# A planner that counts device-memory transfers as longer, and loads that come behind the query unit's pass

## The chip, the cores and the metric

The kernel runs on one core of one Trainium2 chip. The metric is the time of the program on the device in microseconds; the median of several executions counts. Engines are named as in the profile: PE (TensorE, matmuls), PEld (its weight loads), DVE (VectorE), ACT (ScalarE), POOL (GpSimd) and SP (SyncE, which issues all transfers here).

## The reference

Inputs q, k, v have 8 batches, 8 heads, 576 positions and 64 features, in fp32; w_phi is 64 x 128.

```
def phi(x):
    proj = einsum('bhsd,df->bhsf', x, w_phi)
    proj = proj - max(abs(proj), axis=-1)
    return concatenate([exp(proj), exp(-proj)], axis=-1)
q_p, k_p = phi(q), phi(k)
kv  = einsum('bhsf,bhsd->bhfd', k_p, v);  z = sum(k_p, axis=2)
att = einsum('bhsf,bhfd->bhsd', q_p, kv) / (einsum('bhsf,bhf->bhs', q_p, z) + 1e-6)
x   = att as 4608 tokens x 512          # heads side by side
h   = x @ w_in                          # 512 x 2048
out = (h * tanh(softplus(h))) @ w_out   # Mish, then 2048 x 512
```

## The kernel before, in words

Two things run interleaved on one core: linear attention, and the two matrix products with Mish between them.

The 4608 tokens are cut into 18 chunks of 256 (`NCH`, `CH`). For each chunk there are 16 input tiles (`ff_in`, L435: 12 matmuls each, since weight and x are each split into a high and a low part), 8 Mish steps on pairs of tiles (`mish`, L448), the low part of the result (`g_low`, L457) and 16 output tiles (`ff_out`, L470). An input-tile pair writes one of two banks of h; Mish reads it and so frees it.

Attention is cut into units of 512 columns: 36 key units (`k0`...) and 36 query units (`q{chunk}_{g}`). A key unit is loaded (`load_raw`, L250), projected (`project`, L260), centred on VectorE (`centre`, L268), exponentiated on ScalarE (`k_exp`, L322) and summed with v into kv (`k_sum`, L327). Each of the 32 pairs p of heads has its own v (`load_v`, L313). A query unit is loaded, projected and centred likewise. Its features must then be turned over: for the first three chunks by TensorE transposes (`q_turn`), from chunk 3 on (`NTURNED`, query unit 6 on) by a pass through device memory: VectorE regroups 32 x 32 blocks (`q_regroup`), SP sends 256 KB to a scratch tensor (`q_send`, L297) and fetches it back turned in four transfers of 64 KB (`q_fetch`, L302), for each of the two halves j of the unit. Exponentials (`q_exp`, L355), products with kv (`q_num`), the division (`q_divide`) follow, and the result x makes the same pass (`x_regroup`, `x_send`, `x_fetch`), after which ScalarE casts its high part (`q_high`, L423) and VectorE forms its low part (`q_low`, L429). A chunk's first input tile needs x of both its units.

A step takes one query unit and, five steps ahead, one key unit: in step n, projection of query unit n and key unit n + 5, and 8 input and 8 output tiles.

The order of the instructions on each engine isn't that of the code. The class `Plan` (L48) makes it. Each task has an engine, a key (its priority), an assumed duration `took`, an assumed delay `late` until others see its end, tasks it depends on (`deps`: they must have ended; `after`: they must only have been issued), and ring slots that it takes and gives back. `order` (L60) plays the program through in assumed time: a free engine takes the ready task with the lowest key, ScalarE preferring within 1.5 of key one that needs no other activation table. The sequence of issue is then the program's order; each engine runs its instructions in that order, and on the chip waits for what each really needs. For transfers the planner keeps a bus: `size` bytes at 400 KB per assumed microsecond, with a start delay, and a least time until the data count as landed (L104 to L106). SP's `took` is 0.42 for one transfer and 1.68 for the four of a fetch.

The first loads and the weights' tasks have handwritten keys (`FIRST_KEYS`, `FIRST_QUERIES`, `WKEYS`); from query unit 6 on keys come from `step_time` (L504), 8 to a step. `unit_tasks` (L515) adds the load, projection and centring of a unit.

Of the kernel before, what the change touches and what calls it, by code (L numbers as in the profile page):

```python
# [24 lines left out]
NCH = NTOK // CH  # L25
# [9 lines left out]
NTURNED, NTHERE, EARLY, RAMP = 3, 8, 2.042, (5, 4)  # L35

NK, LEAD = B * NHP * S // 512, 5
# [10 lines left out]
class Plan:  # L48
# [4 lines left out]
    def add(self, name, engine, key, took, fn, deps=(), take=(), give=(), late=0.15, table=None, size=0,  # L53
            after=()):
        task = dict(name=name, engine=engine, key=key, took=took, fn=fn, deps=deps, take=take, give=give, late=late,
                    table=table, size=size, after=after, seq=len(self.tasks))
        self.tasks.append(task)
        self.named[name] = task

    def order(self):  # L60

        waiting = {}
        for task in sorted(self.tasks, key=lambda t: (t["key"], t["seq"])):
            waiting.setdefault(task["engine"], []).append(task)
        free = dict.fromkeys(waiting, 0.0)
        done, slots, released = {}, {}, {}
        now, table, bus = 0.0, None, 2.5
        issued = []

        def ready(task):  # L70
            if any(dep not in done for dep in task["after"]):
                return False
            for dep in task["deps"]:
                if done.get(dep, 1e9) > now:
                    return False
            for ring, _ in task["take"]:
                held_now = sum(released.get(token, 1e9) > now for token in slots.setdefault(ring, []))
                if held_now + sum(r == ring for r, _ in task["take"]) > self.rings.get(ring, 1):
                    return False
            return True  # L80

        while any(waiting.values()):
            moved = False
            for engine, queue in waiting.items():
                if free[engine] > now or not queue:
                    continue
                found = None
                for task in queue[:48]:
                    if found and task["key"] > found["key"] + 1.5:
                        break  # L90
                    if not ready(task):
                        continue
                    if found is None:
                        found = task
                    if task["table"] in (None, table):
                        found = task if found["table"] not in (None, table) else found
                        break
                if found is None:
                    continue
                took, late = found["took"], found["late"]  # L100
                if found["table"] not in (None, table):
                    table = found["table"]
                    took += 1.29
                if found["size"]:  # L104
                    bus = max(bus, now + 0.9) + found["size"] / 400e3
                    late = max(bus - now, 1.9) - took  # L106
                for ring, token in found["take"]:
                    slots[ring] = [t for t in slots[ring] if released.get(t, 1e9) > now]
                    slots[ring].append(token)
                free[engine] = now + took  # L110
                done[found["name"]] = now + took + late
                for token in found["give"]:
                    released[token] = now + took + late
                issued.append((now, len(issued), found))
                queue.remove(found)
                moved = True
            if not moved:
                times = [t for t in list(free.values()) + list(done.values()) if t > now + 1e-9]
                if not times:
                    raise RuntimeError("the plan is stuck: " + ", ".join(q[0]["name"] for q in waiting.values() if q))  # L120
                now = min(times)
        return [task for _, _, task in issued]
# [3 lines left out]
def attention_then_mish(ctx, tc, qT, kT, va, w_phi, w_in, w_out, out):  # L126
# [123 lines left out]
    def load_raw(unit, home, src):  # L250
        slot, half = home
        if half is None:
            raws[unit] = work.tile([P, 512], F32, tag="raw", name=f"raw_{unit}", bufs=NRAW)
        else:
            if half == 0:
                shared[slot] = slot_tile(slot, F32, f"raw_{unit}")
            raws[unit] = shared[slot][:, half, :]
        nc.sync.dma_start(raws[unit], src)
# [54 lines left out]
    def load_v(p):  # L313
        if p < NHP:
            vt = spare_tile(NRAWSPARE // 2 + p, F32, f"v_{p}").rearrange("p a b -> p (a b)")
            vt = vt[:, :10 * VW].rearrange("p (t j w) -> p t j w", t=5, j=2)
        else:
            vt = work.tile([P, 5, 2, VW], F32, tag="v", name=f"v_{p}", bufs=NV)
        nc.sync.dma_start(vt.rearrange("p t j w -> p (t j w)"), va[p])
        vs[p] = vt  # L320
# [186 lines left out]
    add = plan.add  # L507
# [7 lines left out]
    def unit_tasks(unit, step, t, load, src, kinds, size):  # L515
        home, e_homes = raw_home(), [e_home(), e_home()]
        slot, half = home
        token = f"raw:{unit}" if half is None else f"{slot}:{shared_by.setdefault(slot, unit)}"
        take = [] if half == 1 else [(slot, token)]
        add(f"load {unit}", "SP", load, 0.42, lambda: load_raw(unit, home, src), take=take, size=size)  # L520
        last_use.setdefault(slot, []).append(f"project {unit}")
        for h in e_homes:
            last_use.setdefault(h, []).append(f"sum {unit}" if unit[0] == "k" else f"num {unit} 1")
        add(f"project {unit}", "PE", t, 1.0, lambda: project(unit, kinds), deps=[f"load {unit}"], after=sums_at.get(step - 1, ()),
            take=[(kind, f"pp{j}:{unit}") for j, kind in enumerate(kinds)], give=[token] if half != 0 else [])
        add(f"centre {unit}", "DVE", t, 2.4, lambda: centre(unit, e_homes), deps=[f"project {unit}"],
            take=[(h, f"e{j}:{unit}") for j, h in enumerate(e_homes)], give=[f"pp{j}:{unit}" for j in range(2)])

    shared_by, last_use, sums_at = {}, {}, {}
    units = sorted([(t, 0, n) for n, t in key_time.items()] + [(t, 1, n) for n, t in query_time.items()])  # L530
    for t, is_query, n in units:
        steady = t >= query_time[NFIRST]
        first = t < 0
        load = (-40.0 + t if t < -3 else -46.6 + 0.2 * t) if first else t - 4.0
        exps = (t + 8 * E0, t + 8 * (E0 + E1)) if steady else (t + 0.3, t + 0.5)
        sums = step_time((n if is_query else n - LEAD) + 1) - 0.03 if steady else t + 1.0
        if not is_query:
            unit = f"k{n}"
# [4 lines left out]
            deps, take, give, ends = [f"exp {unit} 0", f"exp {unit} 1"], [], [], []  # L543
            cost = 0.1
            for i in range(4):
                for p, slot in pairs_of(4 * n + i):
                    cost += 0.466
                    if slot == 0:
                        take.append(("o" if p < NHP else "att", f"kvps:{p}"))
                        vslot = spare[NRAWSPARE // 2 + p] if p < NHP else "v"  # L550
                        add(f"load v{p}", "SP", load + 0.3, 0.42, lambda p=p: load_v(p), take=[(vslot, f"v:{p}")], size=337920)
                        deps.append(f"load v{p}")
                    if slot == 4:
                        last_use.setdefault(spare[NRAWSPARE // 2 + p] if p < NHP else "v", []).append(f"sum {unit}")
                        ends.append(p)
                        give.append(f"v:{p}")
# [7 lines left out]
        else:  # L564
            c, g = divmod(n, 2)
            unit = f"q{c}_{g}"
# [3 lines left out]
            for j in range(2):  # L570
                if by_dma:
                    add(f"regroup {unit} {j}", "DVE", t + 0.1, 0.68, lambda c=c, g=g, j=j: q_regroup(c, g, j), deps=[f"centre {unit}"])
                    add(f"send {unit} {j}", "SP", t + 0.3, 0.42, lambda c=c, g=g, j=j: q_send(c, g, j), deps=[f"regroup {unit} {j}"],
                        size=262144)
                    add(f"turn {unit} {j}", "SP", t + 0.8, 1.68, lambda c=c, g=g, j=j: q_fetch(c, g, j), deps=[f"send {unit} {j}"],
                        size=262144)
# [3 lines left out]
                turn = exps[j] if steady else t + 0.1 + 0.1 * j  # L580
                add(f"turn {unit} {j}", "PE", turn, 0.4, lambda c=c, g=g, j=j: q_turn(c, g, j), deps=[f"centre {unit}"],
                    take=[("att", f"dt{j}:{unit}")])
# [4 lines left out]
            for i in range(2):  # L587
                pair = 2 * g + i
                if steady:
# [3 lines left out]
                    take=[("att", f"num{i}:{unit}")],  # L593
# [11 lines left out]
            else:  # L605
                add(f"out {unit}", "PE", outs, 0.4, lambda c=c, g=g: q_out(c, g), deps=[f"divide {unit} {i}" for i in range(2)],
                    take=[("att", f"xt:{unit}")], give=[f"x:{unit}"])
# [5 lines left out]
    for i, pc in enumerate(pieces):  # L613
# [5 lines left out]
        if i < nmiddle:  # L619
            home = homes[i % len(homes)]  # L620
# [3 lines left out]
        def split(step, took, fn, deps, **more):  # L624
# [5 lines left out]
              take=[("part", f"rest:{nm}"), ("half", f"t:{nm}")] if own else [])  # L630
# [11 lines left out]
    for n in range(total):  # L642
        c, f = tiles[n]
        deps = [f"{s} {('in', cc, f // 4)}" for cc in range(NCC) for s in ("ready", "split")] + [f"low q{c}_{g}" for g in range(2)]
        add(f"in {c} {f}", "PE", n, 1.405, lambda c=c, f=f: ff_in(c, f), deps=deps + ([before_in] if before_in else []),
            take=[] if f % 2 else [("h", f"h:{c}_{f // 2}")], give=[f"xT:q{c}_{g}" for g in range(2)] if f == NFT - 1 else [])
        before_in = f"in {c} {f}"
        if f % 2:
            fp = f // 2
            add(f"mish {c} {fp}", "ACT", n + 0.01, 1.05, lambda c=c, fp=fp: mish(c, fp), deps=[before_in],  # L650
                take=[("u", f"u:{c}_{fp}"), ("g", f"g0:{c}_{fp}"), ("g", f"g1:{c}_{fp}")], give=[f"h:{c}_{fp}"], table="mish")
            add(f"low {c} {fp}", "DVE", n + 0.02, 0.67, lambda c=c, fp=fp: g_low(c, fp), deps=[f"mish {c} {fp}"], give=[f"u:{c}_{fp}"])
        part, first, end = part_of(c, f)
        if f == end - 1:
# [6 lines left out]
            take=[("o", f"o{tt}:{c}_{part}") for tt in range(2)] if f == first else [], give=gives)  # L661
        before_out = f"out {c} {f}"
        if f == end:
            for tt in range(2):
                final = f == NFT - 1
                on_act = c == NCH - 1 and final and not tt or part == 0 and not final
                if part == 0 and not final:
                    take = [("part", f"part{tt}:{c}")]
# [44 lines left out]
```

## Time and profile before

| | |
|---|---|
| median of 3 runs | 1114.09 us (1109.9 to 1115.74) |
| the profiled execution | 1113.29 us |
| its span, first to last instruction | 1111.5 us |
| granted TensorE clock, mean | 0.993 |
| mean DMA rate over the span | 108 GB/s |
| x sends (`there_x`), median from issue to landing | 3.0 us |
| e_q sends (`there_e`), median from issue to landing | 2.2 us |
| raw_k loads, median from issue to landing | 2.9 us |
| v loads, median from issue to landing | 3.7 us |

The page gives for each engine its busy time and share of the span; the stretches give the same for parts of the span (busy us and instructions of PE, PEld, DVE, ACT, POOL, then the granted clock, the DMA engines' share and GB/s). A line of the waits names the waiting engine, its tile and line, the one that it waited for, and then the total in us, the number of times and the longest. A line of a timeline has start and duration in us, engine, source line, operation, output, input, shapes, how many were merged, and in brackets the idle time before it and what ended it.

### The profile page before, as it was taken

Reading aid. Unit: us, or ns where it says so; the run is one execution under the profiler, and the core shown is the slowest. Engines: PE = TensorE matmul, PEld = TensorE weight load, DVE = VectorE, ACT = ScalarE, POOL = GpSimd, SP = SyncE. Lnnn points to the kernel's source line nnn. Section 1 sums busy time; section 2 is a strip of 40 time slices with the busy share of each in tenths; the row PEclk is TensorE's granted clock in tenths of the full one; section 3 lists DMA queues with packets and bytes.
Section 4 is the critical chain, followed back from the end, with each engine's and each line's share of the span. In section 5 each row is a group of like instructions: output and inputs, shape, how many; then the busy total and the mean of one; then the engine's idle time right before and its main releaser. Section 6 shows DMA issues by size and latency. Waiting matters only on the chain.

```text
span 1111.5 us, 26782 instructions
## 1 busy us (share of the span) xinstructions
PE 1074.4 (97%) x11272; PEld 963.0 (87%) x11272; DVE 537.2 (48%) x1184; ACT 657.7 (59%) x1007; POOL 0.7 (0%) x6
## 2 busy tenths in 40 slices
PE   7799999999999999999999999999999999999998
PEld 7689988998898888888888988889899988999887
DVE  7899996444444444333444444444444443433211
ACT  6498996555555556666666665566666563443422
POOL 0000000000000000000000000000000000000000
PEclk9899999999999999999999999999999999999999
DMA  9568743233332322222232322232322221322100
GB/s 352 190 228 287 268 137 105 77 109 108 89 108 89 102 65 88 80 81 88 77 108 89 108 89 96 85 104 77 103 74 93 88 85 58 99 78 76 44 21 19
DMA packets 94008, 120.10 MB, mean 108 GB/s; under 512 B 10432, under 2 KB 56640, under 8 KB 93888
## 3 DMA queue, kind: packets, MB, share of 16 engines
q1 hardware_dynamic: 93888, 118.38, 32.5%
q8 instruction: 89, 1.46, 0.5%
q14 instruction: 31, 0.25, 0.1%
HBM read 85.31 MB, written 33.03 MB: 106 GB/s over the span
## 4 chain that ended last, share of the span: by engine, by line
PE 64%; ACT 14%; DMA 10%; DVE 6%; SPq 3%; issue 3%; ACTq 0%; DVEq 0%
PE h L445 24%; PE o L480 23%; PE kvps L289 7%; PE num L289 6%; DMA there_x<-via 4%; ACT L451 3%; DMA x<-there_x 3%; SPq L302 2%; PE pp_q L266 2%; DMA e_q<-there_e 2%; PE pp_k L266 2%; ACT L355 2%; ACT u L451 1%; ACT e_k L324 1%; ACT L324 1%
## 5 line engine op out<-in xcount | busy, mean ns | idle before, releaser
L445 PE MATMUL h<-xTh,win 128*128 128x256 f32 x2304 | 463.9, 284 | 19.0 <-ACT u L451 16.4
L445 PEld LDWEIGHTS h<-xTh,win 128*128 128x128 f32 x2304 | 374.3, 189 | 45.7 <-ACT u L451 28.8
L480 PE MATMUL o<-wout,gh 128*128 128x512 f32 x1152 | 363.7, 397 | 0.2 <-ACT wout L234 0.2
L445 PE MATMUL h<-xTl,win 128*128 128x256 f32 x1152 | 325.1, 282 | 0.9 <-DVE xTl L429 0.9
L462 DVE TENSOR_TENSOR gl<-u,gh 128x256 fp32r<-128x256 f32 x288 | 110.0, 422 | 420.6 <-ACT gh L454 402.5
L480 PE MATMUL o<-wout,gl 128*128 128x512 f32 x576 | 227.2, 394 | 0.0
L445 PEld LDWEIGHTS h<-xTl,win 128*128 128x128 f32 x1152 | 216.8, 188 | 10.4 <-DVE xTl L429 1.5
L480 PEld LDWEIGHTS o<-wout,gh 128*128 128x128 f32 x1152 | 197.7, 188 | 30.0 <-ACT wout L234 0.6
L451 ACT ACTIVATE u<-h 128x512 f32<-128x512 f32 x144 | 86.1, 598 | 104.4 <-PE h L445 88.7
L423 ACT CAST xTh<-x 128x512 fp32r<-128x512 f32 x30 | 18.7, 622 | 199.6 <-DMA x<-there_x 199.6
L480 PEld LDWEIGHTS o<-wout,gl 128*128 128x128 f32 x576 | 108.3, 188 | 26.4
L451 ACT ACT_TABLE_LOAD x91 | 116.8, 1283 | 1.6
L454 ACT CAST gh<-u 128x256 fp32r<-128x256 f32 x288 | 104.1, 405 | 6.1
L324 ACT ACT_TABLE_LOAD x36 | 46.2, 1283 | 87.3 <-DVE e_k L281 86.8
L289 PEld LDWEIGHTS kvps<-v,e_k 128*64 128x64 f32 x2560 | 79.5, 139 | 8.6 <-issue 5.5
L289 PE MATMUL kvps<-v,e_k 128*64 128x66 f32 x2560 | 84.4, 225 | 0.7 <-issue 0.6
L289 PE MATMUL num<-kv,e_q 128*64 128x66 f32 x2304 | 76.8, 225 | 0.5 <-ACT e_q L360 0.5
L289 PEld LDWEIGHTS num<-kv,e_q 128*64 128x64 f32 x2304 | 72.6, 140 | 4.1 <-issue 1.8
L355 ACT ACT_TABLE_LOAD x42 | 53.9, 1283 | 9.5 <-DMA e_q<-there_e 8.8
L429 DVE TENSOR_TENSOR xTl<-x,xTh 128x512 fp32r<-128x512 f32 x30 | 20.8, 693 | 63.8 <-ACT xTh L423 63.8
L273 DVE TENSOR_REDUCE m_k<-pp_k 128x4 f32<-128x512 f32 x72 | 46.1, 681 | 8.8 <-PE pp_k L266 8.7
L324 ACT ACTIVATE e_k<-e_k 128x512 f32<-128x512 f32 x72 | 45.1, 626 | 6.5 <-DVE e_k L281 6.1
(59 smaller groups left out, 774.9 us busy)
## 6 DMA issues: line engine op xcount, KB each, us to landing
there_e<-e_q SPq DMA_DIRECT2D x60, 256.0 KB, 2.2
e_q<-there_e SPq DMA_DIRECT2D x240, 64.0 KB, 2.0
v<-va SPq DMA_DIRECT2D x32, 330.0 KB, 3.7
raw_q<-qT SPq DMA_DIRECT2D x36, 256.0 KB, 3.2
out<-osb SPq DMA_DIRECT2D x36, 256.0 KB, 2.3
raw_k<-kT SPq DMA_DIRECT2D x35, 256.0 KB, 2.9
words_in<-w_in SPq DMA_DIRECT2D x16, 512.0 KB, 5.9
words_out<-w_out SPq DMA_DIRECT2D x16, 512.0 KB, 4.9
```

The source lines that it names most:

```text
L266: nc.tensor.matmul(ps[j][:, n], raw[rows, n * P:(n + 1) * P], w_phi2[rows], start=True, stop=True)
L273: nc.vector.tensor_reduce(ms[j], ps[j], axis=AX.X, op=ALU.max, apply_absolute_value=True)
L289: nc.tensor.matmul(ps[rows], lhsT[h], rhs[h], start=start, stop=stop, skip_group_check=True)
L302: nc.sync.dma_start(dst[32 * b:32 * b + 32].rearrange("i (a m) -> i a m", a=4), src[:, b * P:(b + 1) * P].rearrange("(a i) m -> i a m", a=4))
L324: nc.scalar.activation(e[:, 1, :], e[:, 0, :], AF.Exp)
L355: nc.scalar.activation(e[:, 1, :], e[:, 0, :], AF.Exp)
L429: nc.vector.tensor_sub(natural(lo), xt_ps.pop((c, g)), natural(hi).bitcast(F32))
L445: nc.tensor.matmul(ps, w[:, wcol], x[:, cc % 2, :], start=(n == 0), stop=(n == 11))
L451: nc.scalar.activation(u, h_live.pop((c, fp)).rearrange("p f s -> p (f s)"), AF.Mish)
L454: nc.scalar.copy(gh, u[:, f * CH:(f + 1) * CH])
L462: nc.vector.tensor_sub(gl, u[:, f * CH:(f + 1) * CH], gh.bitcast(F32))
L480: nc.tensor.matmul(ps, g[:, cols], w, start=(i == first and k == 0), stop=(i == end and k == 2))
```

## The change

The planner's cost of a transfer is changed in two numbers: the bus starts it 1.0 after its issue in place of 0.9, and the data count as landed no sooner than 2.4 after the issue's end (`took`), where it was 1.9 after the issue's start. Nothing else in the planner is touched. And loads of raw inputs and of v get an `after`: from step 7 to step 35 they may be issued only when the second fetch (j = 1) of the query features of the step before has been issued. Loads of weights, and sends and fetches themselves, get no `after`.

```
-                    bus = max(bus, now + 0.9) + found["size"] / 400e3
-                    late = max(bus - now, 1.9) - took
+                    bus = max(bus, now + 1.0) + found["size"] / 400e3
+                    late = max(bus - now - took, 2.4)
...
-        add(f"load {unit}", "SP", load, 0.42, lambda: load_raw(unit, home, src), take=take, size=size)
+        add(f"load {unit}", "SP", load, 0.42, lambda: load_raw(unit, home, src), take=take, size=size, after=turned_at(step - 1))
...
+    def turned_at(step):
+        return [f"turn q{step // 2}_{step % 2} 1"] if 2 * NTURNED <= step < 2 * NCH else []
...
-                        add(f"load v{p}", "SP", load + 0.3, 0.42, lambda p=p: load_v(p), take=[(vslot, f"v:{p}")], size=337920)
+                        add(f"load v{p}", "SP", load + 0.3, 0.42, lambda p=p: load_v(p), take=[(vslot, f"v:{p}")], size=337920,
+                            after=turned_at(n - LEAD - 1))
```

## The prediction

> **What bounds the kernel now.** I read the page's busy shares and chain first, then the waits, then the stretches of the span, then the timelines of two steps that behave differently.
>
> ```profile
> span 1111.5 us, 26782 instructions
> ...
> PE 1074.4 (97%) x11272; PEld 963.0 (87%) x11272; DVE 537.2 (48%) x1184; ACT 657.7 (59%) x1007; POOL 0.7 (0%) x6
> ...
> PE 64%; ACT 14%; DMA 10%; DVE 6%; SPq 3%; issue 3%; ACTq 0%; DVEq 0%
> ```
>
> TensorE has work for all but 37.1 us of the span (1111.5 - 1074.4), so no change of order can win more than that. Yet a quarter of the chain that ended last is ACT and DMA (14% and 10%). The waits say where those touch TensorE:
>
> ```profile
> ACT xTh L423 <- DMA x<-there_x: 199.6, 30, 12.6
> ...
> PEld h L445 <- ACT u L451: 28.8, 31, 2.2
> ...
> PE h L445 <- ACT u L451: 16.4, 22, 1.7
> ...
> PE h L445 <- DVE xTl L429: 0.9, 3, 0.3
> ```
>
> ScalarE sits 199.6 us, 30 times, in front of the cast of x, waiting for x to come back from device memory. Whatever is written behind that cast in ScalarE's order waits with it, Mish (L451) too, and TensorE's input tiles wait 31 times for Mish, because Mish frees the bank of h that they write. The stretches show that this isn't everywhere:
>
> ```profile
> 20.00:40.00 20.00, 17.81 (x395) 16.39 (x390) 15.02 (x40) 9.69 (x18) 0.00 (x0) 0.91 0.58 217
> 40.00:60.00 20.00, 14.78 (x192) 13.78 (x191) 18.32 (x45) 12.01 (x20) 0.00 (x0) 0.83 0.74 255
> ...
> 400.00:500.00 100.00, 96.33 (x1113) 86.12 (x1112) 43.60 (x98) 58.05 (x88) 0.00 (x0) 1.00 0.28 85
> ...
> 800.00:900.00 100.00, 100.00 (x1025) 90.44 (x1024) 43.24 (x92) 63.94 (x93) 0.00 (x0) 1.00 0.30 95
> ```
>
> From 400 to 500 TensorE is idle 3.67 us, from 800 to 900 not at all, with the same kind of steps in both. The difference is in the order. A step of the first kind, by SyncE's, VectorE's, ScalarE's and TensorE's timelines:
>
> ```profile
> 528.61 0.35 SPq L258 DMA_DIRECT2D raw_k<-kT  x1
> 529.11 0.34 SPq L297 DMA_DIRECT2D there_x<-via  x1
> 529.63 0.33 SPq L258 DMA_DIRECT2D raw_q<-qT  x1
> 532.08 1.75 SPq L302 DMA_DIRECT2D x<-there_x  x4
> ...
> 536.88 3.64 SPq L302 DMA_DIRECT2D e_q<-there_e  x8
> ```
> ```profile
> 528.37 0.71 DVE L293 STREAM_TRANSPOSE via<-x 128x512 f32<-128x512 f32 x1
> ...
> 532.57 1.27 DVE L281 TENSOR_TENSOR e_k<-pp_k,m_k 128x512 f32<-128x512 f32 x2
> ...
> 537.00 0.69 DVE L429 TENSOR_TENSOR xTl<-x,xTh 128x512 fp32r<-128x512 f32 x1 [1.95 <-ACT xTh L423]
> ```
> ```profile
> 536.35 0.62 ACT L423 CAST xTh<-x 128x512 fp32r<-128x512 f32 x1 [11.48 <-DMA x<-there_x]
> 536.99 1.28 ACT L324 ACT_TABLE_LOAD   x1
> 538.28 0.64 ACT L324 ACTIVATE e_k<-e_k 128x512 f32<-128x512 f32 x1
> 538.95 0.63 ACT L325 ACTIVATE e_k<-e_k 128x512 f32<-128x512 f32 x1
> 539.60 1.28 ACT L451 ACT_TABLE_LOAD   x1
> 540.89 0.60 ACT L451 ACTIVATE u<-h 128x512 f32<-128x512 f32 x1
> ...
> 547.35 0.60 ACT L451 ACTIVATE u<-h 128x512 f32<-128x512 f32 x1
> ```
> ```profile
> 505.20 0.40 PE L480 MATMUL o<-wout,gl 128*128 128x512 f32 x1
> 505.44 0.28 PE L445 MATMUL h<-xTh,win 128*128 128x256 f32 x1
> ...
> 540.65 0.40 PE L480 MATMUL o<-wout,gl 128*128 128x512 f32 x1
> 541.54 0.39 PE L445 MATMUL h<-xTh,win 128*128 128x256 f32 x1 [0.50 <-ACT u L451]
> ...
> 547.05 0.39 PE L480 MATMUL o<-wout,gl 128*128 128x512 f32 x1
> 548.00 0.39 PE L445 MATMUL h<-xTh,win 128*128 128x256 f32 x1 [0.56 <-ACT u L451]
> ```
>
> VectorE ends the regroup of x at 529.08 (528.37 + 0.71); the cast runs at 536.35, 7.27 us later. The exponentials of the key unit were ready from 533.84 (532.57 + 1.27) and stood behind the cast. An unhindered change from output to input matmuls takes 0.24 us from start to start (505.20 to 505.44); here it takes 0.89 and 0.95, so this step loses 0.65 + 0.71 = 1.36 us. The row's own 0.50 and 0.56 are too small, since a matmul's recorded duration covers part of the gap. The weight loads' row is too large by about 0.28 each (its wait at 547.99 is 0.99 for a loss of 0.71), so the whole loss is 28.8 - 31 x 0.28 = 20.1 us.
>
> The Trainium skill ("Perfetto Trace Analysis", section "Identifying the Most-Contended Engine") holds that matmul busy time is a poor measure of headroom and that the busy share of weight loads should be taken. By that rule 148.5 us (1111.5 - 963.0) would be open to a change. The trace doesn't bear that out for a change of order: between 800 and 900 nothing waits and weight loads still stand at 90.44%.
>
> A step of the second kind:
>
> ```profile
> 564.47 0.70 DVE L293 STREAM_TRANSPOSE via<-x 128x512 f32<-128x512 f32 x1
> ```
> ```profile
> 564.04 1.28 ACT L324 ACT_TABLE_LOAD   x1 [8.77 <-DVE e_k L281]
> ...
> 570.52 0.62 ACT L423 CAST xTh<-x 128x512 fp32r<-128x512 f32 x1 [1.24 <-DMA x<-there_x]
> ...
> 658.76 0.62 ACT L423 CAST xTh<-x 128x512 fp32r<-128x512 f32 x1 [2.33 <-DMA x<-there_x]
> ```
> ```profile
> 660.16 0.38 PE L445 MATMUL h<-xTl,win 128*128 128x256 f32 x1 [0.23 <-DVE xTl L429]
> ```
>
> Here exponentials and a Mish stand ahead of the cast, ScalarE waits only 1.24 us for x, and TensorE doesn't wait for Mish. The pass took 5.35 us (565.17 to 570.52). In exchange x comes just in time where it opens a new chunk (660.16, 0.23 us late).
>
> **The change part by part.** The planner's numbers decide only the order in which each engine's instructions are written; the times below are the trace's.
>
> *Transfers counted as longer.* Before, a 256 KB transfer with the bus free is planned as done 1.9 us after its issue, so send and fetch take 3.8 us. Now it is its issue time plus 2.4: 0.42 + 2.4 = 2.82 for a send, 1.68 + 2.4 = 4.08 for a fetch, together 6.9 us. The chip takes 7.27 in the first kind of step and 5.35 in the second, so the old plan was short by 3.5 and 1.6 us, and the new one is off by -0.4 and +1.6.
>
> What the planner then puts ahead of the cast is what is ready in those 3.1 us: the table load with the first exponential pair (1.28 + 0.64 + 0.63 = 2.55 us), or the Mish that is due. In the step shown ScalarE would start the pair at 533.84 and end it at 536.4, just when x is there; the cast follows to 537.0, the table load for Mish to 538.3. Mish runs at about 538.4 instead of 540.89, 2.5 us earlier. What is late next is the following Mish: 6.46 us separate the two (540.89 to 547.35), because table loads and exponentials lie between, while TensorE needs one per two tile pairs, 5.75 us (548.00 - 541.54, less the 0.71 it waited). So ScalarE loses 0.7 us of its lead per such cycle, and 2.5 us hold for this step. The longest single loss in the trace is 2.2 - 0.28 = 1.9 us, below that lead. I credit 19 of the 20.1 us.
>
> What it may cost: at a chunk's first input tile x has no time in hand in steps of the second kind. If the cast stands behind another pair, 2.55 us, of which ScalarE spends 2.33 idle anyway (658.76), the cast is about 0.2 us late; with a fetch planned longer than it is, up to 1.6 us later. Fifteen chunks begin that way, at 0 to 1.6 us each; most steps of the first kind have 541.54 - 537.69 = 3.85 us in hand and pay nothing. I take 2 us in all, bounds 0 and 24. For such cycles that bunch up (0.7 us each) I take another 2, bounds 0 and 10.
>
> *The same numbers in the ramp.* The first 60 us are bound by arrivals and by handwritten keys: idle 2.19 and 5.22 us in the two stretches above. There a raw load is now planned 0.92 us later (2.82 for 1.9), a weight piece 0.6 later (2.82 for 2.21) when the bus is free.
>
> ```profile
> words_in<-w_in SPq DMA_DIRECT2D x16, 512.0 KB, 5.9
> raw_q<-qT SPq DMA_DIRECT2D x36, 256.0 KB, 3.2
> ```
>
> Both really land later than either plan says, so the new order should be nearer the truth, but no row shows what it will be. Bounds: half of the two idle stretches won, -4 us; two tile pairs of 2.8 us delayed, +6. I take 0.
>
> *Loads behind the query unit's pass.* From step 7 on raw q, raw k and v are loaded after the second fetch of the query features of the step before. The loads leave their place around the send of x (528.61 and 529.63 around 529.11; the fetch that needs the landing starts at 532.08, 2.97 us after the send). SyncE's queue: what they pass is the send and fetch of x, the two sends and eight fetch instructions of e_q; no load's wait for a projection then stands in front of these. Cost: in each step they are issued some 12 us later, at 540.5 (536.88 + 3.64). They are used by the next projection:
>
> ```profile
> 558.18 1.16 PE L266 MATMUL pp_q<-w_phi,raw_q 64*128 64x128 f32 x16
> ```
>
> 540.5 + 3.2 is 543.7, so 14 us remain, and I cost the move at nothing; without that cover each step would pay up to 3.2 us. Its gain, x some 0.9 us sooner, goes into ScalarE's lead and isn't counted again; bounds 0 and 1.
>
> The Trainium skill says the contrary of this move ("DMA: Bandwidth & Descriptors", section "Rules for kernel authors"): issue a transfer early and wait for it late, so that its fixed cost is hidden. By that rule the later issue is a loss. The trace shows it still hidden by 14 us, so both come to nothing here.
>
> **Sum.** -19 + 2 + 2 + 0 = -15 us on the profiled execution's 1113.29 us (span 1111.5 and 1.8 around it): 1098.3. That execution lies 0.8 below the median of 1114.09, so I forecast 1099.0.
>
> **The rivals.** *Same time: the loss comes back elsewhere.* ScalarE needs 6.46 us for a Mish with a table turn, TensorE 5.75. If query features, now planned 3.1 us later, make three turns out of two in a step, 0.7 us in each of 30 steps gives 21 us back against 19, and where only half the steps do it, 10: 1104 to 1116. For it: from 536.35 to 541.49 ScalarE runs without a gap in the step shown. Against it: from 800 to 900 the same work goes by without idle time on TensorE.
>
> *Slower: x comes too late for its chunk.* If the longer plan puts a further table turn ahead of the cast in steps of the second kind, the first input tile of a chunk waits 2.55 us, 15 times: +38 - 19 = +19, so 1133. It decides once the cast is over 1.3 us late per chunk on average (19 / 15). For it: 660.16 shows no time in hand. Against it: x is ready at a lower key than the second exponential pair, and a cast needs no table, so the planner prefers it; and in the first kind 3.85 us are free.
>
> *The change does nothing.* If the planner's order on ScalarE stays, because TensorE's own pace decides when tasks are ready, only x's 0.9 us remain: a gain below 0.65 us per step in some 14 steps, 1105 to 1114.
>
> **How the numbers follow.** Forecast 0.6, with its own range 1091 to 1107 (all of the 20 us and a ramp 4 better; half of it and a ramp worse). Loss comes back 0.15; nothing 0.1; slower 0.15. The range takes the forecast, both middle cases and the lesser part of the slow one: 1091 to 1121. A measurement here can tell 0.5%, 5.6 us, from no change: faster is below 1108.5, which holds the forecast and some of both middle cases (0.04), 0.64; slower is above 1119.7, the slow rival and a ramp that goes wrong without a gain behind it (0.02), 0.17; the rest is 0.19.
>
> **What would show it.** Right: ScalarE's wait at the cast falls from 199.6 us to under 60, with exponentials or Mish ahead of it in every step; input tiles wait for Mish under 10 times over 0.35 us; TensorE's idle time from 200 to 1050 falls by over 10 us; the raw loads stand behind the eight fetches on SyncE, and fetches of x start about 2 us after the send. Wrong: long waits of input tiles for VectorE's low part of x (the slow rival), ScalarE without a gap but TensorE still waiting for Mish (loss comes back), or a first 170 us that is longer by more than the rest wins.

## The result, and the profile after

The changed kernel takes 1082.85 us (median of 4 runs, 1081.57 to 1083.76) against 1112.53 us before (4 runs, 1109.9 to 1115.74): a ratio of 0.9731 with a 95% interval of 0.97 to 0.9762, so 29.7 us less. The forecast had the direction and the place, but half the size: 1099.0, some 15 us less, with a range that ended at 1091.

The page of the changed kernel, the lines that answer to those shown of before (busy time of the engines, and the chain that ended last):

```profile
span 1080.5 us, 26883 instructions
...
PE 1061.9 (98%) x11272; PEld 963.2 (89%) x11272; DVE 539.9 (50%) x1184; ACT 666.3 (62%) x1013; POOL 0.7 (0%) x6
...
PE 89%; ACT 6%; DVE 3%; issue 1%; DMA 1%; SPq 0%; ACTq 0%; DVEq 0%
```

TensorE is now 89% of the chain (64% before), and DMA went from 10% to 1%. Note that TensorE's busy time fell too, by 12.5 us, though it runs the same 11272 matmuls: part of what was lost before had been counted as busy. The waits of the changed kernel:

```profile
ACT L324 <- DVE e_k L281: 201.9, 22, 10.0
...
ACT xTh L423 <- DMA x<-there_x: 15.2, 10, 3.1
...
PEld h L445 <- ACT u L451: 1.5, 1, 1.5
```

ScalarE's wait for x fell from 199.6 us to 15.2. ScalarE still idles, but now mostly in front of the key unit's exponentials (201.9 us), at a time when no Mish is due: in the step shown below the pair of input tiles that the next Mish reads is complete only at 515.35, after the idle time has ended. Input tiles waited 31 times for Mish and now once, at 160.93, before the steady steps. The two stretches that were compared before:

```profile
400.00:500.00 100.00, 100.00 (x1028) 91.15 (x1027) 42.25 (x92) 67.96 (x100) 0.00 (x0) 1.00 0.32 102
...
800.00:900.00 100.00, 100.00 (x1011) 91.05 (x1008) 45.57 (x96) 61.02 (x91) 0.00 (x0) 1.00 0.29 94
```

TensorE has no idle time left in either. A step of the changed kernel on ScalarE and on SyncE, which answers to the one shown at 528 us of before:

```profile
514.79 1.28 ACT L324 ACT_TABLE_LOAD   x1 [9.56 <-DVE e_k L281]
516.09 0.63 ACT L324 ACTIVATE e_k<-e_k 128x512 f32<-128x512 f32 x1
516.75 0.63 ACT L325 ACTIVATE e_k<-e_k 128x512 f32<-128x512 f32 x1
517.29 0.60 ACT L423 CAST xTh<-x 128x512 fp32r<-128x512 f32 x1
517.91 1.28 ACT L451 ACT_TABLE_LOAD   x1
519.21 0.60 ACT L451 ACTIVATE u<-h 128x512 f32<-128x512 f32 x1
```

```profile
510.58 0.33 SPq L297 DMA_DIRECT2D there_x<-via  x1
512.64 2.66 SPq L302 DMA_DIRECT2D x<-there_x  x4
...
521.88 0.37 SPq L258 DMA_DIRECT2D raw_k<-kT  x1
522.35 0.37 SPq L258 DMA_DIRECT2D raw_q<-qT  x1
```

The pair of exponentials stands ahead of the cast, and the cast doesn't wait. Counted from the send of x, Mish starts 8.63 us later (519.21 - 510.58); before it was 11.78 (540.89 - 529.11). The raw loads come behind the fetches.

The span is 31.0 us shorter. Marking in both traces where query units 6, 7 and 31 are projected splits this (units count from 0; the first features are sent at 168.89, and unit 6 is the first that makes the pass, so the projection at 160.00 is unit 6's). First the marks of before, then those of the changed kernel:

```profile
160.00 1.16 PE L266 MATMUL pp_q<-w_phi,raw_q 64*128 64x128 f32 x16
...
168.89 1.25 SPq L297 DMA_DIRECT2D there_e<-e_q  x2
...
197.83 1.16 PE L266 MATMUL pp_q<-w_phi,raw_q 64*128 64x128 f32 x16
...
912.75 1.16 PE L266 MATMUL pp_q<-w_phi,raw_q 64*128 64x128 f32 x16
```

```profile
157.56 1.16 PE L266 MATMUL pp_q<-w_phi,raw_q 64*128 64x128 f32 x16
...
193.08 1.16 PE L266 MATMUL pp_q<-w_phi,raw_q 64*128 64x128 f32 x16
...
884.96 1.16 PE L266 MATMUL pp_q<-w_phi,raw_q 64*128 64x128 f32 x16
```

Up to the projection of unit 6 every engine has the same instructions in the same order, and 2.4 us there are a difference between two executions, none of the change's. From there to unit 7 are 2.3 us: the planner ordered the last weights otherwise, and a wait of input tiles for a weight (2.8 us in the weight loads' row) is gone. Not all of the 2.3 need be the change's: a kernel of the experiments whose instructions are those of before up to there took 36.9 us for the 37.8. The 24 steps to unit 31 took 714.9 and now 691.9: 23.0. The rest, to the end, gives 3.2.

### The profile page after: what moved, and what is told of

It reads as the page before. It is cut to its first block, busy times and chain, and to the rows that moved or that the text cites. A ratio compares the mean times of both kernels' runs of the same rounds, so it can differ in the third digit from the quotient of the medians.

```text
span 1080.5 us, 26883 instructions
## 1 busy us (share of the span) xinstructions
PE 1061.9 (98%) x11272; PEld 963.2 (89%) x11272; DVE 539.9 (50%) x1184; ACT 666.3 (62%) x1013; POOL 0.7 (0%) x6
## 4 chain that ended last, share of the span: by engine, by line
PE 89%; ACT 6%; DVE 3%; issue 1%; DMA 1%; SPq 0%; ACTq 0%; DVEq 0%
PE h L445 34%; PE o L480 34%; PE kvps L289 7%; PE num L289 6%; PE pp_q L266 3%; PE pp_k L266 3%; ACT L451 1%; ACT u L451 1%; ACT wout L234 1%; ACT L182 1%; PE dt L350 0%; ACT gh L454 0%; DMA raw_k<-kT 0%; ACT w_out L182 0%; ACT e_q L360 0%
## 5 line engine op out<-in xcount | busy, mean ns | idle before, releaser
L480 PEld LDWEIGHTS o<-wout,gh 128*128 128x128 f32 x1152 | 197.3, 188 | 29.3 <-ACT wout L234 1.3
L324 ACT ACT_TABLE_LOAD x50 | 64.2, 1283 | 202.4 <-DVE e_k L281 201.9
L324 ACT ACTIVATE e_k<-e_k 128x512 f32<-128x512 f32 x72 | 45.3, 629 | 8.3 <-DVE e_k L281 7.8
L266 PE MATMUL pp_k<-w_phi,raw_k 64*128 64x128 f32 x560 | 44.5, 292 | 4.5 <-DMA raw_k<-kT 4.5
L325 ACT ACTIVATE e_k<-e_k 128x512 f32<-128x512 f32 x72 | 45.5, 632 | 2.3
L266 PEld LDWEIGHTS pp_k<-w_phi,raw_k 64*128 64x128 f32 x560 | 40.8, 201 | 6.0 <-issue 4.8
```

The lines of the kernel that those rows point to most:

```text
L266: nc.tensor.matmul(ps[j][:, n], raw[rows, n * P:(n + 1) * P], w_phi2[rows], start=True, stop=True)
L324: nc.scalar.activation(e[:, 1, :], e[:, 0, :], AF.Exp)
L325: nc.scalar.activation(e[:, 0, :], e[:, 0, :], AF.Exp, scale=-1.0)
L480: nc.tensor.matmul(ps, g[:, cols], w, start=(i == first and k == 0), stop=(i == end and k == 2))
```

## The experiments

Ten more kernels were timed, each beside the kernel before on the same chip (medians of 1113.1 to 1114.4 us there; the ratios below are to these). Two of them leave out the fetch of x, so that x enters the products unturned; they serve only to see where the time goes. One table first, worked out from TensorE's timelines: when query unit 7 is projected (the expectations for two of the runs call this mark unit 6), how long the next 24 steps take, how many input tiles of these start over 0.16 us later than usual behind an output tile and what all entries behind output tiles lose over the usual 1.39 us from start to start, and how often TensorE switches between attention's matmuls and the products' tiles.

| kernel | median us | unit 7 at | 24 steps | late entries, us | switches |
|---|---|---|---|---|---|
| before | 1112.53 | 197.8 | 714.9 | 20, 18.3 | 68 |
| after | 1082.85 | 193.1 | 691.9 | 0, 0.6 | 50 |
| planner's numbers only | 1083.07 | 195.3 | 691.9 | 0, 0.6 | 50 |
| moved loads only | 1102.34 | 195.8 | 707.3 | 15, 11.0 | 66 |
| numbers for passes only | 1090.21 | 195.9 | 696.5 | 0, 1.5 | 90 |
| numbers for loads only | 1125.29 | 199.4 | 724.3 | 33, 28.2 | 50 |
| before, x not fetched | 1088.41 | 195.8 | 694.6 | 1, 2.0 | 68 |
| x alone planned later | 1098.18 | 196.5 | 699.8 | 4, 3.6 | 90 |
| 3.2 for 2.4 | 1084.94 | 192.6 | 692.5 | 0, 0.7 | 54 |
| 4.8 for 2.4 | 1096.14 | 196.6 | 700.9 | 0, 1.7 | 119 |
| loads' numbers, x not fetched | 1090.17 | 198.1 | 694.4 | 3, 2.5 | 50 |
| 2.0 for 2.4 | 1084.18 | 195.5 | 691.9 | 0, 0.6 | 50 |

The theory was the prediction's: the planner takes the pass of x for too short, writes its cast too early in ScalarE's order, and Mish waits behind it. The rival was that the moved loads, which shorten the pass, make the gain.

**Which half of the change does it.** The changed kernel without the `after` of the loads (v's likewise):

```
-  ... take=take, size=size, after=turned_at(step - 1))
+  ... take=take, size=size)
```

> The planner's two new numbers, loads left without their after. If the cast's place in ScalarE's order is the cause: steady stalls go as in the changed kernel, input tiles wait for Mish under 3 us in total, and the time is 1083 to 1088, with sends of x still taking 3 to 5 us until their fetch where raw loads stand around them. If the moved loads are the cause (the pass made about 1 us shorter): the time stays at 1105 to 1113.

1083.07 us, a ratio of 0.9734 (0.9708 to 0.976) to before: as the changed kernel. On TensorE, VectorE and ScalarE it has the changed kernel's instructions in the changed kernel's order, and the 24 steps are equal to the tenth of a microsecond.

```profile
ACT xTh L423 <- DMA x<-there_x: 28.0, 18, 5.3
...
PEld h L445 <- ACT u L451: 1.5, 1, 1.5
```

The other half alone, with the old two lines in the planner:

> The loads moved behind the pass, the planner's numbers as before. If the cast's place is the cause: ScalarE still waits over 150 us for x, each wait about 1 us shorter, and input tiles still wait for Mish; each of some 14 steps wins at most 1 us, so 1098 to 1112. If the moved loads are the cause: 1083 to 1090, with sends of x at 2.0 to 2.1 us until their fetch.

1102.34 us (0.9898; 0.9869 to 0.9928). Sends of x are now 2.0 to 2.1 us from their fetch in 23 of 30 passes (3 to 5 in the first kind of step before), so the loads had been in their way, and the pass is about 1 us shorter in steps of the first kind. ScalarE still waits at the cast:

```profile
ACT xTh L423 <- DMA x<-there_x: 152.1, 25, 11.9
ACT xTh L423 <- DVE e_q L293: 51.3, 5, 11.8
...
PEld h L445 <- ACT u L451: 17.7, 25, 1.4
```

203.4 us of waiting, and 11.0 us of late entries in place of 18.3. So the moved loads win 1% alone, because x comes sooner to a cast that stands too early: up to 607 us the order on the compute engines is still that of before. They win nothing measurable on top of the planner's numbers. The rival falls as an account of the change, and the prediction's price for the move (0, bounds 0 and 1) holds only in combination.

**Is it the wait, or the order?** The kernel before, unchanged in the order of its compute engines, with nothing fetched for x:

```
 def x_fetch(c, g):
     x = x_live.pop((c, g)).rearrange("p i t m -> p (i t m)")
-    fetch(f"x_{c}_{g}", x)
+    there.pop(f"x_{c}_{g}")
```

> The kernel before in its own order, with the four fetches of x left out: x is sent, but the cast reads x where the division wrote it, so the attention result enters the products unturned. Only the wait goes, no instruction on ScalarE, VectorE or TensorE moves. If ScalarE's wait at the cast is what delays Mish, input tiles wait for Mish under 3 us in total and the steady part is some 22 to 26 us shorter: 1086 to 1092. If the stall comes from the order of table loads and exponentials itself, whatever x does: 1104 to 1113, with waits for Mish as before.

1088.41 us (0.977; 0.9738 to 0.9802).

```profile
ACT xTh L423 <- DVE x L395: 55.3, 14, 5.7
...
PEld h L445 <- ACT u L451: 2.5, 4, 1.2
```

TensorE, VectorE and ScalarE run the same instructions in the same order as before, and the stall goes when the wait goes: 31 waits for Mish become 4, and 20 late tiles in the 24 steps become 1. This shows the cause. (What stands behind the fetches in SyncE's queue comes sooner too, which this run doesn't separate.)

**Which transfers have to be counted longer.** The new numbers for sends and fetches of passes alone, and for loads and stores alone, both without `after` (the second has `not in` for `in`):

```
+  if found["name"].split()[0] in ("send", "turn", "out"):
       bus = max(bus, now + 1.0) + found["size"] / 400e3
       late = max(bus - now - took, 2.4)
+  else:
+      bus = max(bus, now + 0.9) + found["size"] / 400e3
+      late = max(bus - now, 1.9) - took
```

> New numbers for sends and fetches of the passes alone, loads and stores planned as before, no after. Passes begin with query unit 6, so the ramp up to there should be as before: if ramp and steady part are separate, the first projection of query unit 6 stays at about 197.8 us, the rest is 26 us shorter, and the time is 1086 to 1090. If the gain of 4.8 us before that point also comes from passes, it is 1082 to 1085.

1090.21 us (0.979; 0.9758 to 0.9823), unit 7 at 195.9 instead of the expected 197.8. That is no gain of the passes': unit 6 comes 1.6 us sooner already, where the order is that of before, and from unit 6 to unit 7 it takes 37.5 us for 37.8. No input tile is late in the 24 steps, yet the 24 steps take 4.6 us more than in the changed kernel. They have 90 switches against 50.

> New numbers for loads and stores alone, passes planned as before, no after. If the loads' numbers make the ramp's gain and the passes' numbers the rest: first projection of query unit 6 at about 193 us, waits at the cast of x and for Mish as before, time 1105 to 1110. If loads' numbers also set the steady order: under 1100.

1125.29 us, slower than before (1.0112; 1.0081 to 1.0143), and unit 7 at 199.4, not 193. That was a miss: neither theory had it. Its waits (code lines are 4 higher here):

```profile
ACT xTh L427 <- DMA x<-there_x: 295.6, 30, 13.2
...
PEld h L449 <- ACT u L455: 41.5, 39, 2.2
```

With loads planned longer, nearly every step becomes of the first kind, where both projections run together and x is regrouped ahead of the centring. That order has the fewest switches (50), and it is the one in which the too early cast costs most. To see whether that is all, the same kernel without the fetches of x:

> The kernel with the loads' new numbers alone, which waits for Mish in every step with key units (35 late tile entries, about 31 us over the usual), and with the four fetches of x left out, so that the attention result enters the products unturned. The order of no compute engine moves. If the wait for x makes these stalls, and switches of TensorE between attention and tiles (49 from 200 to 900 us, as in the changed kernel) the rest: about 34 us less than with the fetches, 1087 to 1093, and 24 steps in about 692 us, as in the changed kernel. If the order with the loads' numbers is slow for another reason: over 1100.

1090.17 us (0.9796; 0.9763 to 0.9829); late entries 2.5 us in place of 28.2, the 24 steps 694.4 and, less the late entries, what the changed kernel has. So the two parts of the new numbers work together: loads counted longer make the order of each step compact, passes counted longer put the cast where it doesn't wait. Either alone has a price that the other takes away.

**The cast alone.** Before, with one line behind the old two:

```
+  late += 3.1 if found["name"].startswith("out q") else 0.0
```

> The planner's old numbers, but the fetch of x alone counted as landing 3.1 us later; everything else, the loads too, as before. If the cast's place is all: about 1087 to 1092, no wait for Mish over 0.5 us, cast of x behind an exponential pair in every step with key units. If the features' pass or the loads have to be planned longer too: over 1095.

1098.18 us (0.9861; 0.9829 to 0.9892): half of the gain. Late entries fall to 3.6 us in the 24 steps, but there are 90 switches, and beyond unit 31 three input tiles wait for Mish or x again (one 1.39 us for Mish; two that open a chunk take 2.5 and 2.6 us). So "the cast's place is all" is wrong: the order that the other transfers set counts too.

**How long is right.** The changed kernel with other values for the least time (3.2 here; also 2.0 and 4.8):

```
-                    late = max(bus - now - took, 2.4)
+                    late = max(bus - now - took, 3.2)
```

> The changed kernel with 3.2 in place of 2.4: a send planned at 3.62, a fetch at 4.88, the pass of x at 8.5 us, longer than the 5.4 to 7.2 that it takes. By the order theory there are 3.9 us in hand between the low part of x and a chunk's first tile, so the same time as the changed kernel within 0.4%: 1079 to 1087. If a plan that is too long costs at once (x late for its chunk): over 1092, with tiles that wait for VectorE's low part.

> The changed kernel with 2.0 in place of 2.4: the pass of x planned at 2.42 + 3.68 = 6.1 us, above the 5.4 that a quiet pass takes and below the 6.7 at which the changed kernel runs its cast. If what counts is that the planned pass isn't shorter than the real one: 1081 to 1087. If the planner needs the full 6.9 to put an exponential pair ahead of the cast: waits for x return and the time is 1090 to 1108.

> The changed kernel with 4.8: the pass of x planned at 11.7 us, beyond the time in hand. If the slow rival is real, casts now stand behind a further table turn and chunk starts wait about 2.5 us each, 15 times: 1100 to 1125. If the planner fills the time with output tiles and nothing is lost: 1080 to 1090.

2.0 gives 1084.18 us (0.9737; 0.9699 to 0.9775), 3.2 gives 1084.94 (0.9744; 0.9707 to 0.9781), both like 2.4 within what can be told. 4.8 gives 1096.14 (0.9843; 0.9811 to 0.9874), between its two expected ranges: about 13 us of the 30 go back, 9.0 of them in the 24 steps. But not in the way that the slow rival has it:

```profile
ACT xTh L423 <- DMA x<-there_x: 0.9, 1, 0.9
...
PEld h L445 <- DVE xTl L429: 0.5, 1, 0.5
...
PEld h L445 <- ACT u L451: 0.5, 1, 0.5
```

Next to nothing waits for x, its low part or Mish, though two exponential pairs now stand ahead of most casts. The time of the 24 steps is in the order: TensorE's timeline of this kernel, and below it that of the changed one (only the first matmuls of each group are shown).

```profile
540.84 1.16 PE L289 MATMUL num<-kv,e_q 128*64 128x66 f32 x32
541.92 0.39 PE L445 MATMUL h<-xTh,win 128*128 128x256 f32 x1
...
543.54 1.16 PE L289 MATMUL num<-kv,e_q 128*64 128x66 f32 x32
...
544.62 0.39 PE L445 MATMUL h<-xTh,win 128*128 128x256 f32 x1
...
546.24 1.16 PE L266 MATMUL pp_q<-w_phi,raw_q 64*128 64x128 f32 x16
```

```profile
506.88 2.05 PE L289 MATMUL num<-kv,e_q 128*64 128x66 f32 x64
508.86 1.16 PE L266 MATMUL pp_q<-w_phi,raw_q 64*128 64x128 f32 x16
509.85 1.23 PE L266 MATMUL pp_k<-w_phi,raw_k 64*128 64x128 f32 x16
511.01 0.39 PE L445 MATMUL h<-xTh,win 128*128 128x256 f32 x1
...
512.54 0.62 PE L480 MATMUL o<-wout,gh 128*128 128x512 f32 x2
513.93 0.28 PE L445 MATMUL h<-xTh,win 128*128 128x256 f32 x1
...
515.35 0.62 PE L480 MATMUL o<-wout,gh 128*128 128x512 f32 x2
```

With 4.8 the planner, waiting for late transfers, puts input tiles between the two halves of the numerator's products. Such a tile takes 1.62 us (541.92 to 543.54; 544.62 to 546.24), one among the products' tiles 1.42 (513.93 to 515.35), and the numerator's 64 matmuls take 1.08 twice in place of 1.98. By this, each change between the two kinds of matmul costs about 0.1 us, and no wait is recorded for it. Over the kernels of the table, the 24 steps less their late entries, and less what input tiles ahead of an output tile take over 1.42 us, are 689.0 us at 50 switches, 691.0 at 68, 693.1 at 90 and 696.8 at 119: 0.11 us per switch. This is a fit over whole orders; no run varies the switches alone.

## Why the prediction was right in direction and wrong in size

- The cause was named rightly: the wait at the cast of x, Mish behind it, the bank of h. The kernel before without the fetch shows it. The step shown went as worked out: Mish was put at 538.4 us, 9.3 after the send, and came 8.63 after it. The signs of success came: the wait under 60 us, an exponential pair ahead of the cast in 24 of the 30 passes and a Mish in the other six, loads behind the fetches, and TensorE's idle time between 200 and 1050 us gone altogether.
- What failed is the sum. First the term "the whole loss is 20.1 us, I credit 19", which was sized from the rows of waits and so too small. Counted by TensorE's starts from unit 7 to the end, entries lost 22.1 us over the usual, of which the changed kernel keeps 0.8. Input tiles also ran over the usual 1.42 us, by 6.4 us in all before and 2.9 after. Of the 6.4, 4.4 are in tiles behind an output tile that entered late (some by under 0.16 us) or, at three chunk starts, were held up inside; the rest, and all of the 2.9, is in tiles right behind attention's matmuls. Together 24.8 us were won. The range's end at 1091 allowed for all of the 20 us and 4 of the ramp, and so rests on the same term. Nor were TensorE's 37.1 us without work the most that an order can win: its busy time fell by 12.5 us. The tile at 541.54 of before took 1.54 us where an undisturbed one takes 1.42:

```profile
538.07 0.28 PE L445 MATMUL h<-xTh,win 128*128 128x256 f32 x1
...
539.49 0.63 PE L480 MATMUL o<-wout,gh 128*128 128x512 f32 x2
...
543.08 0.62 PE L480 MATMUL o<-wout,gh 128*128 128x512 f32 x2
```

- Second, the two costs of 2 us each, for x late at chunk starts and for table turns that bunch up, didn't come: input tiles wait for x's low part once, 0.3 us, and for Mish not once in the steady steps. ScalarE does make six table loads more (175 for 169, in front of Mish and of the exponentials of L324 and L355), but in time that was idle.
- Third, a term was missing: the step shown as the good kind, with waits for nothing, has a tile between the two projections (558.18 and 560.88), and pays for it in switches. The changed kernel has 18 fewer in the 24 steps, 2.0 us at 0.11; more of its input tiles stand right behind attention's matmuls, and with these counted the gain is 1.3 us (the kernel before without the fetch, less its late entries, takes 692.6 us, the changed kernel 691.3). I took the stretch without idle time for the best that there is; the changed kernel's steps are still 0.4 us shorter (28.9 for 29.3).
- Fourth, the ramp. In the first 60 us, which that term was about, the change moves no instruction, so the 0 there is right for another reason than the one given (a new order nearer the truth). What was won, up to 2.3 us, comes between units 6 and 7, where the sum had no term. Another 2.4 us of the span's difference aren't the change's.
- The rivals. Loss that comes back elsewhere: TensorE has no idle time from 200 to 1050 us that would show it. The change does nothing: excluded. Slower by x that comes too late for its chunk: not even at 4.8, since the planner then fills TensorE with other tiles; what an overlong plan costs is switches.

Open is why the planner, once loads count longer, writes both projections together: presumably by its bookkeeping of banks and ready times, which no run here takes apart.

## What to carry to other kernels

Where one host-side plan writes the order of in-order engines, an assumed latency that is too short is paid twice: the consumer waits, and so does everything written behind it. Take the latency from the trace of the pass as it runs in the kernel, not of one transfer; a value somewhat too long (here 2.0 to 3.2 for the least time) costs nothing, one far too long splits work into pieces and costs that. And when a change has several parts, measure each alone: one of them here, the longer count for loads, lost 1% by itself and is needed for the best time.

## What the runs showed of the hardware that was not expected

- Changing TensorE between attention's matmuls (64*128 and 128*64 in the rows) and the products' (128*128) costs about 0.1 us each time, inside what the profile calls busy: with 119 changes for 50, 24 steps took 700.9 us in place of 691.9, with TensorE at 100% from 200 to 900 us in both. It is a fit (0.11 us) over four counts of changes.
- An input tile that starts late behind a wait takes 1.52 us instead of 1.42 (medians of 20 and 134 tiles in the 24 steps of before), and the matmuls' recorded wait, 0.50 us at 541.54, leaves out part of the gap too (0.65). So the recorded wait understates the loss.
- A 256 KB send with a raw load issued half a microsecond ahead of it and one behind took 3.0 to 5.1 us until its fetch could be issued, and 2.0 to 2.1 in a quiet queue; in some passes of the changed kernel it takes 2.9 to 3.8 though nothing was issued within 4 us ahead of it, and what causes those is open.
